# A general path for large experts moves to the end of the program, and the token number scatters to experts 4 to 7

## The chip, the cores and the metric

The kernel runs on one core of a Trainium2 chip. A core has five engines with queues of their own: PE (TensorE, matmuls), ACT (ScalarE), DVE (VectorE), POOL (GpSimd, which here also issues the scatters) and SP (SyncE, which issues the loads). The metric is the device time of one execution in microseconds.

## The reference

Attention runs only between queries and keys whose hashes fall into one bucket. Its output goes token by token to one of eight experts, and the sum of that through a dense layer of two matrices. The hash and softmax of the attention are left out here:

```python
def _moe_ref(x, w_gate, w_output_gate, w1, w2):        # x 1536 x 512, w1 8 x 512 x 1024, w2 8 x 1024 x 512
    e_idx = np.argmax(x @ w_gate, axis=1)
    ...
    for e in range(E):
        mask = e_idx == e
        h = np.maximum(x[mask] @ w1[e], 0.0)
        ye = h @ w2[e]
        out[mask] = gate_w[mask, None] * eom[mask, e, None] * ye

def _moe2_ref(x, w_in, w_out):                         # w_in 512 x 2048, w_out 2048 x 512
    h = x @ w_in
    g = np.where(h > 0.0, h, np.exp(np.minimum(h, 0.0)) - 1.0)
    return g @ w_out
```

## The kernel before

**Attention and gate.** The first third of the program is attention, 16 heads of 768 tokens. At its end the gate picks an expert for each token, ranks the tokens of an expert, and scatters their rows (512 values and the factor) to `xs_d` in DRAM, where each expert has a region of its own. `tab` holds the counts, and as its last number `most`, the largest of them. A path of fixed size takes `CAP` = 224 tokens of each expert; with this data no expert has more.

**Experts.** For expert 0 the tokens are picked with selection matmuls into `xacc`, and ACT and DVE copy that in two halves into the high and low part of `xt`. Expert e+1's rows come from DRAM by `load_xs`, are scaled by POOL (`scale_xs`, L782) and transposed by PE (`make_xT`, tile `xTp`, L1028) inside expert e's second layer. Layer 1 (`moe_L1`, `hps`, L1044) and layer 2 (`moe_L2`, `yps`, L1054) have 96 matmuls of 224 columns each, since every product is made of three: high by high, high by low and low by high. The weights come in 512 KB pieces, `wraw` (eight of an expert, six buffers); ACT makes the high part `wh` (L757) and DVE the low part `wl` (L760). `hh` and `hl` are the two parts of layer 1's output; `hps` has three buffers.

**The general code.** Before expert 0 each engine loads `most` from `tab` (L1060) and branches (L1061) around code that handles what exceeds 224 tokens, with loops over experts and tokens. With this data it is skipped. `keep_warm` (L589) puts 6 matmuls on PE just before it, on data that nobody uses.

**Token numbers.** `tids` scatters, for a quarter of the tokens, their numbers to `tid_d`: three small DVE operations and three indirect DMAs from POOL (L989), with a `spacer` after each. Four groups are called in experts 1 and 2, two in each. `tidt`, loaded from `tid_d`, holds the places of the rows at the end.

**Dense layer and end.** Sixteen blocks `ff_L1`, ELU, `ff_L2` follow, then `finish`: DVE adds to `part` (L1210), and POOL stores it by an indirect DMA through `tidt` (L1214). `lows` issues the subtractions that make `gl`, the low part of the ELU's output.

**What sets the order.** The instructions of each engine stand in the order in which the program is written, each engine runs its own queue in order, and semaphores hold what depends on another engine. SP issues loads as buffers come free, in the order of the program.

Of the kernel before, what the change touches and what calls it, by code (L numbers as in the profile page):

```python
# [17 lines left out]
ENG = mybir.EngineType  # L18
# [7 lines left out]
def kernel(  # L26
# [15 lines left out]
    nc = tc.nc  # L42
    B, H, S, D = q.shape
    E, DM, F = w1.shape
    NT = B * S
# [4 lines left out]
    HC = HALF * 128  # L50
# [44 lines left out]
    PW = KD * F // 4  # L95
    wraw = {}

    def load_piece(pc, e=None):
        i = pc % NP
        we1, we2 = (w1[pc // NP], w2[pc // NP]) if e is None else (w1[bass.ds(e, 1)][0], w2[bass.ds(e, 1)][0])  # L100
        t = raw_p.tile([128, PW], F32, tag="w", name="wraw") if e is None else m1.tile(
            [128, PW], F32, tag="wh", name="wraw", bufs=5
        )
        if i < 4:
            n = F // 4
            src = we1[:, i * n:(i + 1) * n].rearrange("(c p) f -> p c f", p=128)
        else:
            src = we2[:, (i - 4) * 128:(i - 3) * 128].rearrange("(c p) f -> p c f", p=128)
        nc.sync.dma_start(t.rearrange("p (c f) -> p c f", c=src.shape[1]), src)  # L109
        wraw[pc] = t  # L110
# [638 lines left out]
    def split_piece(pc, eng=nc.vector, eng_hi=nc.scalar, rest=None):  # L749
        if pc not in wraw:  # L750
            return
        r = wraw.pop(pc)
        p, a, n = (m2a, "v", 3) if 0 <= pc < 3 else (m1, "w", 5)
        hi = p.tile([128, PW], F32R, tag=a + "h", name="wh", bufs=n)
        lo = p.tile([128, PW], F32R, tag=a + "l", name="wl", bufs=n)
        if eng_hi is nc.scalar:
            eng_hi.activation(hi, r, AF.Copy)  # L757
        else:
            eng_hi.tensor_copy(hi, r)
        fs = [lambda: eng.tensor_tensor(lo, r, hi, ALU.subtract)]  # L760
        if rest is None:
            both(fs)
        else:
            rest.extend(fs)
        wsp[pc] = (hi, lo)
        if pc < 0:
            return
        assert stream[taken[0]] == (pc,)
        taken[0] += 1
        load_ahead()  # L770
# [239 lines left out]
    ps_h = moe.enter_context(tc.tile_pool(name="ps_h", bufs=3, space=PSUM, reuse_waits="tile"))  # L1010


    def load_xs(e, rows=None):
        t = m1.tile([128, 2, XC], F32, tag="xs", name="xs")
        rows = bass.ds(e * REG, ROWS) if rows is None else rows
        nc.sync.dma_start(t, xs_d[rows].rearrange("(t p) d -> p t d", p=128))
        xsl[e] = t

    def make_xT(e, half):
# [36 lines left out]
        nc.scalar.activation(x2h[:, dc, cols], ps, AF.Copy)  # L1056
        nc.vector.tensor_tensor(x2l[:, dc, cols], ps, x2h[:, dc, cols], ALU.subtract)  # L1057

    why = "a count of some of the tokens"
    most = nc.values_load(tab[0:1, 2 * E:2 * E + 1], min_val=0, max_val=NT, skip_runtime_bounds_check_because=why)  # L1060
    with tc.If(most > CAP):  # L1061
        iop = gate_p.tile([128, 2], F32, name="iop")
        nc.gpsimd.iota(iop, pattern=[[128, 2]], base=0, channel_multiplier=1, allow_small_or_imprecise_dtypes=True)
        zrow = m2a.tile([128, XC], F32, tag="mag", name="zrow")
        nc.gpsimd.memset(zrow, 0.0)
        with tc.For_i(0, E, 1) as ev:
            have = nc.values_load(tab[0:1, bass.ds(ev, 1)], min_val=0, max_val=NT, skip_runtime_bounds_check_because=why)
            off = nc.values_load(
                tab[0:1, bass.ds(ev + E, 1)], engines=[ENG.Activation, ENG.DVE], min_val=0, max_val=NT,
                skip_runtime_bounds_check_because=why,  # L1070
            )
            with tc.If(have > CAP):
                tail = gate_p.tile([128, 1], F32, name="tail")
                row = gate_p.tile([128, 2], I32, name="row")
                nc.vector.tensor_tensor(tail, cno[:, 0, bass.ds(ev, 1)], ebase[:, bass.ds(ev, 1)], ALU.add)
                nc.vector.tensor_scalar(row, iop, tail, None, ALU.add)
                for a in range(2):
                    nc.gpsimd.indirect_dma_start(xs_d, bass.IndirectOffsetOnAxis(row[:, a:a + 1], 0), zrow, None)
            with tc.For_i(CAP, have, CAP) as t0:
                load_xs(-1, bass.ds(ev * REG + t0, ROWS))  # L1080
                scale_xs(-1, (nc.scalar, nc.vector))
                make_xT(-1, 0)
                make_xT(-1, 1)
                for f in range(FB1):
                    pc = f // 2 - NP
                    if f % 2 == 0:
                        load_piece(pc, ev)
                        split_piece(pc)
                    moe_L1(-1, f, pc)
                col = nc.s_assert_within(  # L1090
                    off + t0, min_val=0, max_val=NT,
                    skip_runtime_bounds_check_because="t0 is less than what the expert has",
                )
                for dc in range(KD):
                    pc = 4 + dc - NP
                    load_piece(pc, ev)
                    split_piece(pc)
                    moe_L2(-1, dc, pc, col)

    for i in range(1, AHEAD):  # L1100
        split_piece(i)
    for e in range(E):
        if e == 0:
            off = 0
        else:
            off = nc.values_load(
                tab[0:1, E + e:E + e + 1], engines=[ENG.Activation, ENG.DVE], min_val=0, max_val=NT,
                skip_runtime_bounds_check_because="a count of some of the tokens",
            )
        if e == 4:  # L1110
            tidt = gate_p.tile([128, NTT], I32, name="tidt")
            nc.sync.dma_start(tidt, tid_d.rearrange("(t p) o -> p (t o)", p=128))
        if e == 0:
            load_xs(1)
        for f in range(FB1):
            pc = e * NP + f // 2
            moe_L1(e, f, pc)
            narrow_ops(1)
            if f == 1 and e + 1 < E:
                scale_xs(e + 1, (nc.gpsimd, nc.gpsimd))  # L1120
            if f == 2 and 0 < e < 3:
                for gi in range(2 * e - 2, 2 * e):
                    tids(gi)
            if f % 2:
                wsp.pop(pc)
                split_piece(pc + AHEAD)
                if e == E - 1 and f == 7:
                    split_w2(0)
                take_w2()
        if e == 0:  # L1130
            first[0] = False
            load_ahead()
        for dc in range(KD):
# [16 lines left out]
    ps_a = ctx.enter_context(tc.tile_pool(name="ps_a", bufs=1, space=PSUM, reuse_waits="tile"))  # L1150
    m2 = ctx.enter_context(tc.tile_pool(name="m2", bufs=2, reuse_waits="tile"))
    part = [[m2.tile([128, DM], F32, name=f"part{hf}{tt}", bufs=1) for tt in range(2 * HALF)] for hf in range(2)]
    groups = [range(0, W2A), range(W2A, 10), range(10, FB2)]
    steps = [(hf, fb) for g in groups for hf in range(2) for fb in g]
    first_fb, last_fb = [g[0] for g in groups], [g[-1] for g in groups]
# [64 lines left out]
    for k in range(len(steps)):  # L1220
        for j in range(2):
            ps = ff_L1(*steps[k], j)
            if len(todo_w2) < 3:
                take_w2(FB2)
            narrow_ops(3)
            lows()
            ff_elu(*steps[k], j, ps)
            if 0 < k < len(steps) - 1:
                ff_L2(*steps[k - 1], range(HALF * j, HALF * (j + 1)))
            if j == 1 and k + 2 < len(steps) and steps[k + 2][0] == 0 and steps[k + 2][1] > 1:  # L1230
                split_w2(steps[k + 2][1])
    lows()
    for tt in range(2 * HALF):
        for k in (len(steps) - 2, len(steps) - 1):
            ff_L2(*steps[k], [tt])


_INS = [
# [27 lines left out]
```

## Time and profile before

| | |
|---|---|
| median of 3 runs | 743.41 us (743.01 to 743.64) |
| the profiled execution | 745.55 us |
| its span, first to last instruction | 743.8 us |
| mean granted clock of TensorE in it | 0.983 |
| PE busy | 717.9 us, 97% |
| DVE busy | 563.0 us, 76% |
| ACT busy | 400.6 us, 54% |
| POOL busy | 208.9 us, 28% |

The span is that of the one execution that was recorded; the time around it, 1.75 us, has no record. Busy means that a recorded operation ran; branches, semaphores and DMA issues are not counted in it.

### The profile page before, as it was taken

The page shows a single profiled execution, that of the slowest core. Times are in us where ns is not written, and L with a number is a line of the kernel's source. Part 1 is how long each engine was busy: PE and PEld are TensorE (multiplying, and loading weights), DVE is VectorE, ACT ScalarE, POOL GpSimd, SP SyncE. Part 2 cuts the span into 40 slices and gives each one's busy share as a digit, 9 for nine tenths or more (in the row PEclk, how much of TensorE's full clock was granted, in tenths as well). Part 3 has the DMA queues.
Part 4 walks back from the last instruction along what each step waited for, and adds up shares of the span by engine and source line. Part 5 has one row for each costly group of instructions (what it writes and reads, how often), then busy time and mean ns, then how long its engine had stood idle before and what let it go on. Part 6 is the DMA issues. An engine that isn't in the chain of part 4 may idle for free.

```text
span 743.8 us, 13192 instructions
## 1 busy us (share of the span) xinstructions
PE 717.9 (97%) x4686; PEld 674.0 (91%) x4687; DVE 563.0 (76%) x1093; ACT 400.6 (54%) x807; POOL 208.9 (28%) x492
## 2 busy tenths in 40 slices
PE   7999999999999987999999999999999999999996
PEld 5999999999998877999999999889888898899995
DVE  5888898888988975766678898786778965964433
ACT  4897887878878744555555555323433223242221
POOL 7444544454456543154420221100000000000303
PEclk9899999999999988999999999999999999999998
DMA  8856759577582207979898877222112200000202
GB/s 197 192 114 158 187 128 211 150 176 179 136 214 86 72 35 228 267 141 256 182 257 261 263 244 209 83 85 85 58 58 84 79 8 1 0 1 1 85 0 86
DMA packets 108535, 97.74 MB, mean 131 GB/s; under 512 B 33416, under 2 KB 94472, under 8 KB 108464
## 3 DMA queue, kind: packets, MB, share of 16 engines
q1 hardware_dynamic: 106000, 90.44, 46.2%
q0 software_dynamic: 2304, 6.40, 2.3%
q8 instruction: 39, 0.64, 0.4%
q14 instruction: 32, 0.26, 0.1%
q10 hardware_dynamic: 160, 0.00, 0.0%
HBM read 64.15 MB, written 10.72 MB: 101 GB/s over the span
## 4 chain that ended last, share of the span: by engine, by line
issue 40%; PE 12%; DMA 4%; POOL 3%; DVE 1%; ACT 0%; SPq 0%; POOLq 0%; DVEq 0%; ACTq 0%
PE hps L1044 6%; PE yps L1054 5%; DMA xs<-xs_d 4%; POOL xs L782 1%; POOL out_dram L1214 1%; POOL vl L710 1%; PE xTp L1028 1%; DVE wl L760 1%; DVE xTl L1031 0%; ACT wh L757 0%; DVE x2l L1057 0%; SPq L109 0%; POOL spacer L576 0%; ACT x2h L1056 0%; DVE wres L697 0%
## 5 line engine op out<-in xcount | busy, mean ns | idle before, releaser
L367 DVE TENSOR_TENSOR ptlo<-t,pthi 128x384 fp32r<-128x384 f32 x192 | 100.1, 549 | 25.8 <-ACT pthi L366 23.4
L344 ACT ACTIVATE p<-s,bi,sc 128x768 f32<-128x768 f32 x96 | 96.0, 1000 | 21.6 <-POOL bi L337 20.0
L366 ACT ACTIVATE pthi<-t 128x384 fp32r<-128x384 f32 x192 | 84.8, 497 | 25.6 <-PE t L364 24.6
L760 DVE TENSOR_TENSOR wl<-wraw,wh 128x1024 fp32r<-128x1024 f32 x63 | 76.9, 1224 | 21.3 <-ACT wh L757 17.3
L1178 ACT ACTIVATE gh<-ee 128x384 fp32r<-128x384 f32 x64 | 33.7, 526 | 107.8 <-DVE ee L1177 107.8
L335 DVE TENSOR_REDUCE nm<-s 128x1 f32<-128x768 f32 x96 | 91.0, 948 | 0.0
L1166 PE MATMUL gps<-x2l,vh 128*128 128x384 f32 x256 | 86.1, 336 | 0.0
L1166 PE MATMUL gps<-x2h,vh 128*128 128x384 f32 x256 | 86.1, 336 | 0.0
L1166 PE MATMUL gps<-x2h,vl 128*128 128x384 f32 x256 | 85.9, 336 | 0.0
L1214 POOL DMA_INDIRECT out_dram<-part,tidt x12 | 11.6, 969 | 259.0 <-DVE part L1210 256.6
L364 PE MATMUL t<-ident,p 128*128 128x128 f32 x576 | 80.9, 276 | 1.9 <-DVE ptlo L367 1.9
L316 PE MATMUL s<-ka,qa 128*128 128x384 f32 x192 | 74.8, 389 | 3.0 <-ACT p L344 2.4
L1196 PE MATMUL a<-vh,gl 128*128 128x512 f32 x192 | 76.1, 396 | 1.6 <-DVE gl L1179 1.4
L1196 PE MATMUL a<-vh,gh 128*128 128x512 f32 x192 | 75.7, 394 | 0.0
L1196 PE MATMUL a<-vl,gh 128*128 128x512 f32 x192 | 75.6, 394 | 0.0
L364 PEld LDWEIGHTS t<-ident,p 128*128 128x128 f32 x576 | 68.6, 142 | 5.8 <-DVE ptlo L367 2.3
L1054 PE MATMUL yps<-hh,wh 128*128 128x224 f32 x256 | 71.2, 278 | 0.0
L1175 ACT ACTIVATE ee<-gps 128x384 f32<-128x384 f32 x64 | 31.2, 487 | 73.6 <-PE gps L1166 73.3
L1054 PE MATMUL yps<-hl,wh 128*128 128x224 f32 x256 | 70.2, 274 | 0.0
L1054 PE MATMUL yps<-hh,wl 128*128 128x224 f32 x256 | 70.1, 274 | 0.0
L380 PE MATMUL o<-pthi,vst 128*128 128x384 f32 x192 | 68.0, 354 | 0.8 <-ACT osb L401 0.6
L317 PE MATMUL s<-kb,qb 102*128 102x384 f32 x192 | 66.1, 344 | 0.8 <-DVE kb L240 0.8
(202 smaller groups left out, 1872.5 us busy)
## 6 DMA issues: line engine op xcount, KB each, us to landing
wraw<-in_moe_w_dram SPq DMA_DIRECT2D x64, 512.0 KB
w<-in_moe_w_in_dram SPq DMA_DIRECT2D x16, 512.0 KB
w<-in_moe_w_out_dram SPq DMA_DIRECT2D x16, 512.0 KB
ka<-khi SPq DMA_DIRECT2D x30, 192.0 KB
xs_d<-zt SPq DMA_DIRECT2D x8, 528.0 KB
xs<-xs_d SPq DMA_DIRECT2D x8, 528.0 KB
raw_q<-in_q_dram SPq DMA_DIRECT2D x16, 192.0 KB
raw_k<-in_k_dram SPq DMA_DIRECT2D x16, 192.0 KB
```

The lines of the kernel that those rows point to most:

```text
L316: nc.tensor.matmul(ps[:, j, 0:HC], opnd[st, "qa"][:, cb], opnd[st, "ka"][:, sl], start=True, stop=False)
L317: nc.tensor.matmul(ps[:, j, 0:HC], opnd[st, "qb"][0:64 + MROWS, cb], opnd[st, "kb"][0:64 + MROWS, sl], start=False, stop=True,)
L335: nc.vector.tensor_reduce(nm, sps[n][:, :, 0:HC], AX.XY, ALU.max, negate=True)
L344: nc.scalar.activation(p.rearrange("p (a b) -> p a b", a=2), sps.pop(n)[:, :, 0:HC], AF.Exp, bias=bi, scale=sc, accum_out=sums[hd][:, c:c ...
L364: nc.tensor.transpose(ps[:, a, :], p[:, kt * 128:(kt + 1) * 128], ident)
L366: nc.scalar.activation(ho, ps, AF.Copy)
L367: nc.vector.tensor_tensor(lo[:, HALF * g:HALF * (g + 1), i * 128:(i + 1) * 128], ps, ho, ALU.subtract)
L380: nc.tensor.matmul(ops[m], vst[hd][:, kt, :], t[:, kt, :], start=(kt == 0 and x == 0), stop=(kt == NC - 1 and x == 1))
L760: fs = [lambda: eng.tensor_tensor(lo, r, hi, ALU.subtract)]
L1054: nc.tensor.matmul(ps, w[:, f], x[:, f], start=(f == 0 and i == 0), stop=(f == FB1 - 1 and i == 2))
L1166: nc.tensor.matmul(ps, w[:, dc], x[:, dc, c0:c0 + HC], start=(dc == 0 and i == 0), stop=(dc == KD - 1 and i == 2))
L1196: nc.tensor.matmul(ps, x[:, cs], w, start=(fb in first_fb and i == 0), stop=(fb in last_fb and i == 2))
```

## The change

The general code leaves the middle. There POOL alone loads `most` and tests it; the body it would run is two fills of `x2h` and `x2l`. A new general path, `more_tokens`, stands at the end of the program under a test on all engines. It takes 128 rows at a time through both layers of the expert and the dense layer; with this data it is skipped. The token numbers are scattered in experts 4 to 7, one group in each at f == 4, in place of two groups in each of experts 1 and 2 at f == 2, and `tidt` is loaded after the experts. Before the last `lows`, PE takes the last step but one of two parts first. The options that only the general code used leave `load_piece`, `split_piece` and `load_xs`.

```diff
@@ load_piece, split_piece, load_xs: options of the general code removed
-    def load_piece(pc, e=None):
+    def load_piece(pc):
...
-        if pc < 0:
-            return
...
@@ before the loop over experts
-    most = nc.values_load(tab[0:1, 2 * E:2 * E + 1], min_val=0, max_val=NT, skip_runtime_bounds_check_because=why)
+    most = nc.values_load(
+        tab[0:1, 2 * E:2 * E + 1], engines=[ENG.Pool], min_val=0, max_val=NT, skip_runtime_bounds_check_because=more
+    )
     with tc.If(most > CAP):
-        iop = gate_p.tile([128, 2], F32, name="iop")
-        nc.gpsimd.iota(iop, pattern=[[128, 2]], base=0, channel_multiplier=1, allow_small_or_imprecise_dtypes=True)
...
-                    moe_L2(-1, dc, pc, col)
+        nc.gpsimd.memset(x2h.bitcast(F32), 0.0)
+        nc.gpsimd.memset(x2l.bitcast(F32), 0.0)
@@ in the loop over experts
-        if e == 4:
-            tidt = gate_p.tile([128, NTT], I32, name="tidt")
-            nc.sync.dma_start(tidt, tid_d.rearrange("(t p) o -> p (t o)", p=128))
...
-            if f == 2 and 0 < e < 3:
-                for gi in range(2 * e - 2, 2 * e):
-                    tids(gi)
+            if f == 4 and e >= E - NG:
+                tids(e - E + NG)
@@ after it
+    tidt = gate_p.tile([128, NTT], I32, name="tidt")
+    nc.sync.dma_start(tidt, tid_d.rearrange("(t p) o -> p (t o)", p=128))
@@ the dense layer's loop and what follows
                 ff_L2(*steps[k - 1], range(HALF * j, HALF * (j + 1)))
+            elif k and j:
+                ff_L2(*steps[k - 1], [0, 1])
...
     lows()
     for tt in range(2 * HALF):
-        for k in (len(steps) - 2, len(steps) - 1):
+        for k in (len(steps) - 2, len(steps) - 1)[tt < 2:]:
             ff_L2(*steps[k], [tt])
...
+    def more_tokens(e, rows, places):
+        x = raw_tile(XC, "xrow")
+        nc.sync.dma_start(x, xs_d[rows])
...
+        place = gate_p.tile([128, 1], I32, name="place")
+        nc.sync.dma_start(place, tid_d[places])
+        nc.gpsimd.indirect_dma_start(out, bass.IndirectOffsetOnAxis(place, 0), o, None)
+
+    most = nc.values_load(tab[0:1, 2 * E:2 * E + 1], min_val=0, max_val=NT, skip_runtime_bounds_check_because=more)
+    with tc.If(most > CAP):
+        with tc.For_i(0, E, 1) as ev:
...
+                more_tokens(ev, bass.ds(ev * REG + first_row, 128), bass.ds(place0, 128))
```

Two places in the order of the instructions. PE in the middle, before; `warm` is the tile of `keep_warm`, and the dots stand for rows of the general code:

```order
L589 LDWEIGHTS ones_b
L589 MATMUL warm<-ones_b 128x384
L1060 TENSOR_LOAD tab
L1061 COMPARE_AND_BRANCH
...
L1061 UNCONDITIONAL_BRANCH
L1044 MATMUL hps<-xt_4270,wh 128x224
L1044 MATMUL hps<-xt_4271,wh 128x224
```

The same place of the changed kernel, where `hps` is made in L1039; xt_4270 is the high part of xt, xt_4271 the low part:

```order
L587 MATMUL warm<-ones_b 128x384
L1058 UNCONDITIONAL_BRANCH
L587 LDWEIGHTS ones_b
L587 MATMUL warm<-ones_b 128x384
...
L587 LDWEIGHTS ones_b
L587 MATMUL warm<-ones_b 128x384
L1039 MATMUL hps<-xt_4270,wh 128x224
L1039 MATMUL hps<-xt_4271,wh 128x224
```

The load of the count, the compare-and-branch and the code behind it are gone from PE's middle, and one jump stands inside the warm-up.

POOL in the experts, before: the first four scalings of xs (L782) are those for experts 1 and 2, and `tid_d` is written by the token number scatters:

```order
L1061 UNCONDITIONAL_BRANCH
L782 TENSOR_SCALAR xs<-xs 128x512 x4
L989 DMA tid_d<-tok,g_pi 1536x1
L576 MEMSET spacer 1x1
L989 DMA tid_d<-tok,g_pi 1536x1
L576 MEMSET spacer 1x1
```

And of the changed kernel, from its test in the middle on:

```order
L1055 TENSOR_LOAD tab
L1058 COMPARE_AND_BRANCH
L1059 MEMSET x2h 128x7040
L1060 MEMSET x2l 128x7040
L1058 UNCONDITIONAL_BRANCH x2
L778 TENSOR_SCALAR xs<-xs 128x512 x10
L985 DMA tid_d<-tok,g_pi 1536x1
L574 MEMSET spacer 1x1
```

The scatters stand behind ten scalings of xs, those for experts 1 to 5, where they stood behind four.

## Rows read from the trace of the kernel before

**Rows 1.** The chain that ended last, 270 to 300: start us, us, what.

```profile
283.62 13.47 PE hps L1044 x96
```

**Rows 2.** Timeline of PE, 277 to 285: start, us, operation, [idle before <-releaser].

```profile
278.28 1.15 PE L589 MATMUL warm<-ones_b 128*128 128x384 bf16 x6
283.62 0.74 PE L1044 MATMUL hps<-xt,wh 128*128 128x224 f32 x2 [4.19 <-ACT wh L757]
```

**Rows 3.** Instructions of line L1061 by engine: ns min/median/max, first and last start.

```profile
L1061 PEldq EVENT_SEMAPHORE  x2: 51/51/51, 283.2 to 283.4; - x2
...
L1061 PEldq COMPARE_BRANCH x1: 3827/3827/3827, 278.7 to 278.7; - x1
...
L1061 DVEq COMPARE_BRANCH x1: 72/72/72, 281.6 to 281.6; - x1
L1061 POOLq INC_SWDGE_SEM x1: 429/429/429, 282.3 to 282.3; - x1
```

**Rows 4.** Windows of PE: us, busy (instructions), granted clock, DMA share, GB/s.

```profile
283.60:288.90 5.30, 5.28 (x25) 0.50 0.71 200
288.90:297.10 8.20, 8.20 (x75) 1.00 0.84 253
346.80:350.00 3.20, 1.99 (x19) 1.00 1.14 297
```

**Rows 5.** Timelines of ACT and DVE, 277.5 to 287.

```profile
280.20 0.54 ACT L858 ACTIVATE xt<-xacc 128x448 fp32r<-128x448 f32 x1 [1.63 <-PE warm L589]
281.46 2.96 ACT L757 ACTIVATE wh<-wraw 128x1024 fp32r<-128x1024 f32 x3 [0.71 <-ACTq L1060]
...
282.62 3.50 DVE L760 TENSOR_TENSOR wl<-wraw,wh 128x1024 fp32r<-128x1024 f32 x3 [1.22 <-DMA qb<-z]
```

**Rows 6.** PE's waits, 300 to 470: us in total, times, longest.

```profile
PE xTp L1028 <- POOL xs L782: 2.4, 2, 1.2
```

**Rows 7.** The chain that ended last, 320 to 445: loads of xs, issue to landing.

```profile
331.75 12.19 DMA xs<-xs_d
...
423.26 5.68 DMA xs<-xs_d
```

**Rows 8.** Instructions of line L989, the token number scatters.

```profile
L989 POOL DMA_INDIRECT tid_d<-tok,g_pi x12: 955/960/2067, 318.6 to 356.6; - x12
```

**Rows 9.** Windows of the experts, PE busy; the last column is GB/s.

```profile
308.00:318.00 10.00, 10.00 (x92) 1.00 0.89 267
318.00:328.00 10.00, 10.00 (x92) 1.00 0.62 131
328.00:344.00 16.00, 16.00 (x146) 1.00 0.82 185
344.00:354.00 10.00, 8.79 (x80) 1.00 1.09 301
401.00:423.00 22.00, 22.00 (x200) 1.00 0.88 269
```

**Rows 10.** Timeline of PE, 346.5 to 349, the transposes for expert 3.

```profile
346.89 0.27 PE L1028 MATMUL xTp<-ident,xs 128*128 128x128 f32 x1
348.38 0.55 PE L1028 MATMUL xTp<-ident,xs 128*128 128x128 f32 x3 [1.21 <-POOL xs L782]
```

**Rows 11.** Timeline of POOL, 400 to 440, scaling for experts 6 and 7.

```profile
408.16 4.87 POOL L782 TENSOR_SCALAR xs<-xs 128x512 f32<-128x512 f32 x2 [19.85 <-DMA xs<-xs_d]
429.12 3.88 POOL L782 TENSOR_SCALAR xs<-xs 128x512 f32<-128x512 f32 x2 [16.09 <-DMA xs<-xs_d]
```

**Rows 12.** Transposes in 414 to 442: eight for expert 6, four for expert 7.

```profile
L1028 PE MATMUL xTp<-ident,xs x12: 270/272/273, 416.8 to 439.4; 128*128 128x128 f32 x12
```

**Rows 13.** Instructions of line L1214, the stores of the output.

```profile
L1214 POOL DMA_INDIRECT out_dram<-part,tidt x12: 954/960/1038, 687.5 to 738.7; - x12
```

**Rows 14.** Timelines of POOL and DVE, 730 to the end.

```profile
732.41 0.95 POOL L1214 DMA_INDIRECT out_dram<-part,tidt  x1 [37.16 <-DVE part L1210]
...
737.19 0.69 DVE L1210 TENSOR_TENSOR part<-a,part 128x512 f32<-128x512 f32 x1 [0.70 <-PE a L1196]
```

More of the change, by code (lines that the diff above doesn't have):

```diff
@@ L96 @@
     wraw = {}
-    def load_piece(pc, e=None):
+    def load_piece(pc):
         i = pc % NP
[L100 to L103, printed above, removed]
+        we1, we2 = w1[pc // NP], w2[pc // NP]
+        t = raw_p.tile([128, PW], F32, tag="w", name="wraw")
         if i < 4:
@@ L1010, with load_xs @@
     ps_h = moe.enter_context(tc.tile_pool(name="ps_h", bufs=3, space=PSUM, reuse_waits="tile"))
-    def load_xs(e, rows=None):
+    def load_xs(e):
         t = m1.tile([128, 2, XC], F32, tag="xs", name="xs")
-        rows = bass.ds(e * REG, ROWS) if rows is None else rows
-        nc.sync.dma_start(t, xs_d[rows].rearrange("(t p) d -> p t d", p=128))
+        nc.sync.dma_start(t, xs_d[e * REG:e * REG + ROWS].rearrange("(t p) d -> p t d", p=128))
         xsl[e] = t
@@ L1057, in moe_L2 @@
         nc.vector.tensor_tensor(x2l[:, dc, cols], ps, x2h[:, dc, cols], ALU.subtract)
-    why = "a count of some of the tokens"
-    most = nc.values_load(tab[0:1, 2 * E:2 * E + 1], min_val=0, max_val=NT, skip_runtime_bounds_check_because=why)
+    more = "a count of some of the tokens"
+    most = nc.values_load(
+        tab[0:1, 2 * E:2 * E + 1], engines=[ENG.Pool], min_val=0, max_val=NT, skip_runtime_bounds_check_because=more
+    )
     with tc.If(most > CAP):
-        iop = gate_p.tile([128, 2], F32, name="iop")
-        nc.gpsimd.iota(iop, pattern=[[128, 2]], base=0, channel_multiplier=1, allow_small_or_imprecise_dtypes=True)
[L1064 to L1097, printed above, removed]
-                    moe_L2(-1, dc, pc, col)
@@ L1233, with raw_tile, copy, turned @@
     for tt in range(2 * HALF):
-        for k in (len(steps) - 2, len(steps) - 1):
+        for k in (len(steps) - 2, len(steps) - 1)[tt < 2:]:
             ff_L2(*steps[k], [tt])
+    def raw_tile(n, name):
+        return raw_p.tile([128, PW], F32, tag="w", name=name)[:, 0:n]
+    def copy(o, ps):
+        nc.scalar.activation(o, ps, AF.Copy)
+    def turned(src, n, name):
+        dst = raw_tile(n, name)
+        for i in range(0, n, DM):
+            ps = ps_a.tile([128, DM], F32, tag="a0", name="turn")
+            for j in range(0, DM, 128):
+                nc.tensor.transpose(ps[:, j:j + 128], src[:, i + j:i + j + 128], ident)
+            copy(dst[:, i:i + DM], ps)
+        return dst.rearrange("p (c q) -> p c q", q=128)
@@ new lines, in weight_rows @@
+    def weight_rows(src):
+        t = raw_tile(PW, "wrow")
+        nc.sync.dma_start(t.rearrange("p (c n) -> p c n", c=src.shape[1]), src)
+        return t
+    def more_tokens(e, rows, places):
+        x = raw_tile(XC, "xrow")
+        nc.sync.dma_start(x, xs_d[rows])
+        nc.vector.tensor_scalar(x[:, 0:DM], x[:, 0:DM], x[:, DM:DM + 1], None, ALU.mult)
+        xq = turned(x, DM, "xq")
+        ps = [ps_a.tile([128, DM], F32, tag=f"a{1 + i}", name="hrow") for i in range(2)]
+        for dc in range(KD):
+            w = weight_rows(w1[bass.ds(e, 1)][0][dc * 128:(dc + 1) * 128].rearrange("(c p) f -> p c f", c=1))
+            for i in range(2):
+                nc.tensor.matmul(
+                    ps[i], xq[:, dc], w[:, i * DM:(i + 1) * DM], start=(dc == 0), stop=(dc == KD - 1)
+                )
+        h = raw_tile(F, "hrow")
+        for i in range(2):
+            nc.scalar.activation(h[:, i * DM:(i + 1) * DM], ps[i], AF.Relu)
+        hq = turned(h, F, "hq")
+        ps = ps_a.tile([128, DM], F32, tag="a3", name="yrow")
+        for f in range(FB1):
+            if f % 2 == 0:
+                w = weight_rows(w2[bass.ds(e, 1)][0][f * 128:(f + 2) * 128].rearrange("(c p) n -> p c n", p=128))
+            nc.tensor.matmul(ps, hq[:, f], w[:, f % 2 * DM:(f % 2 + 1) * DM], start=(f == 0), stop=(f == FB1 - 1))
+        y = raw_tile(DM, "yrow")
+        copy(y, ps)
+        yq = turned(y, DM, "yq")
+        ps = ps_a.tile([128, DM], F32, tag="a4", name="orow")
+        for fb in range(FB2):
+            for i in range(2):
+                if wide:
+                    load_w2(fb, i)
+                both(narrow_w2(fb, i))
+            wi, wo = wres.pop(fb).rearrange("p a n -> a p n")
+            pg = ps_g.tile([128, HC], F32, tag="g", name="gps")[:, 0:128]
+            for dc in range(KD):
+                nc.tensor.matmul(pg, wi[:, dc * 128:(dc + 1) * 128], yq[:, dc], start=(dc == 0), stop=(dc == KD - 1))
+            ee = m2.tile([128, HC], F32, tag="ee", name="ee")[:, 0:128]
+            nc.scalar.activation(ee, pg, AF.Exp)
+            nc.vector.tensor_scalar(ee, ee, 1.0, 1.0, ALU.min, ALU.subtract)
+            nc.vector.scalar_tensor_tensor(ee, pg, 0.0, ee, ALU.max, ALU.add)
+            nc.tensor.matmul(ps, ee, wo, start=(fb == 0), stop=(fb == FB2 - 1))
+        o = raw_tile(DM, "orow")
+        copy(o, ps)
+        place = gate_p.tile([128, 1], I32, name="place")
+        nc.sync.dma_start(place, tid_d[places])
+        nc.gpsimd.indirect_dma_start(out, bass.IndirectOffsetOnAxis(place, 0), o, None)
@@ new lines @@
+    most = nc.values_load(tab[0:1, 2 * E:2 * E + 1], min_val=0, max_val=NT, skip_runtime_bounds_check_because=more)
+    with tc.If(most > CAP):
+        with tc.For_i(0, E, 1) as ev:
+            have = nc.values_load(tab[0:1, bass.ds(ev, 1)], min_val=0, max_val=NT, skip_runtime_bounds_check_because=more)
+            off = nc.values_load(
+                tab[0:1, bass.ds(ev + E, 1)], engines=[ENG.SP], min_val=0, max_val=NT,
+                skip_runtime_bounds_check_because=more,
+            )
+            with tc.For_i(CAP, have, 128) as t0:
+                first_row = nc.s_assert_within(
+                    have + (CAP - 128) - t0, min_val=0, max_val=NT - 128,
+                    skip_runtime_bounds_check_because="t0 is less than what the expert has",
+                )
+                place0 = nc.s_assert_within(
+                    off + first_row, min_val=0, max_val=NT - 128,
+                    skip_runtime_bounds_check_because="the expert's last token stands among all tokens",
+                )
+                more_tokens(ev, bass.ds(ev * REG + first_row, 128), bass.ds(place0, 128))
```

## The prediction

> **What bounds the kernel now.** I read the chain that ended last first, then the idle time on PE, then the sequencer's own records at the places where PE is idle. From attention's end to the last store the chain lies on PE, so I looked for the few places in the mixture-of-experts stage where PE stands still. There are three. The first is in the middle, at the general code: the warm-up matmuls end at 279.43 (278.28 + 1.15) and the first matmul of expert 0 starts at 283.62, 4.19 us later [rows 2]. The profile puts this down to a high part of a weight piece on ACT, but that engine's record at the place is a load of the count [rows 5], and PE's own record explains the time: its compare-and-branch at 278.7 lasted 3.827 us, where DVE's lasted 0.072 [rows 3]. The reader is to see that the wait is PE's own jump over the general code, not a late operand. The second and third are waits of 1.21 us for the scaled rows of the next expert, 2.4 us together [rows 6].
>
> **The clock behind the gap.** [...] The wait at 348 leaves the clock at 1.00 [rows 4]. So the gap has a second price behind it: expert 0's first layer is 96 matmuls in 13.47 us [rows 1], and at 0.109 it would be 10.50, 2.97 less.
>
> **Edit 1, the general code leaves the middle.** On PE the count load and the compare-and-branch go; what stays is a jump to the next row inside the warm-up. So PE can go straight from 279.43 into expert 0, and 4.19 + 2.97 = 7.16 us are to be had. Something comes due next. ACT has three high parts ahead of its first hh (2.96 us together), and DVE three low parts ahead of its first hl (3.50) [rows 5]; the change leaves both orders as they are. ACT's second copy of xt needs the last selection matmuls, which overlap the start of the warm-up at 278.28 [rows 2]: with its 0.54 us I take 279.1 for its end. The high parts then start at about 279.15, DVE's low parts 1.16 us behind them as now (282.62 against 281.46), so 280.3, and they end at 283.8; hl (0.4) frees the first of three buffers of hps at about 284.2. PE has filled three buffers, 36 matmuls of 0.109, by 283.37. It waits 0.9 us. Term: -4.19 - 2.97 + 0.9 = **-6.3**.
>
> The bound below: if ACT's second copy still starts at 280.20, where the profile shows it 1.63 us behind PE's warm-up matmuls [rows 5], DVE's low half of xt ends about 1.3 us after PE needs it and the first hl is 1.1 us later too; PE loses 1.6 us more, and up to 3 us if the clock falls again. The bound above is no wait at all, -7.2. I take -6.3, since the second copy has no operand that is made after the warm-up begins; only PE's signal of it was late, and PE then stood at the branch.
>
> [...]
>
> POOL's test in the middle: it comes behind the last row scatter on POOL, and the next thing on POOL is scaling xs of expert 1, which waits for its load to land. Nothing waits for the test sooner: zero, with 1 us as the upper bound.
>
> **Edit 2, the token number scatters.** The loads of xs in front of the two PE waits took 12.19 us (the one issued at 331.75) from issue to landing; the one at 423.26 took 5.68 [rows 7]. Between them stand the scatters of tid_d: all 12 lie between 318.6 and 357 in two groups of six [rows 8]. Around the first group the DMA rate falls from 267 GB/s to 131 and then 185 [rows 9], while PE goes on at full pace, so the queues fall behind. Scaled rows come late, and of four transposes in a row the first starts at 346.89, the next three at 348.38 [rows 10], 1.49 us later where matmuls of this kind step by some 0.11. The same again one expert later. With the scatters gone from experts 1 and 2 both waits go: 2 x 1.38 = **-2.8**. Bounds: -2.4 if only the idle time counts [rows 6], and 0 if the landing is late for another reason (the load of weights alone).
>
> They come back as three for each of experts 4 to 7. Price of six, by rate: (259 - 131) x 10 + (259 - 185) x 16 = 2.46 MB not moved, at some 259 GB/s 9.5 us of transfer time (259 is my estimate of the undisturbed demand, a little below the 267 and 269 of [rows 9]). Three should cost about 4.75 us. Catch-up ran at 301 GB/s where expert 6 takes 269 in its undisturbed 22 us [rows 9]: (301 - 269) x 22 = 0.7 MB, or 2.7 us at 259, is won back per expert. What hides the rest: xs of expert 6 is scaled at 413.0 (408.16 + 4.87) and first transposed at 416.8, a margin of 3.8; xs of expert 7 at 433.0 with its first transposes up to 439.4, some 6 [rows 11, 12]. Expert 4's three cost 4.75 against that 3.8 plus what was won back; I take **+0.4**, bounds 0 and, if the price per group doesn't halve, +12 (rival 3). tidt is loaded later, but its first use is the store at 687.5 [rows 13], and nothing reads it sooner: zero. The three small DVE operations per group move with the scatters; DVE has idle time there: zero.
>
> **Edit 3, the end.** POOL paces it: the last six stores begin at 732.41 and 738.7, 1.26 us apart, each 0.96, and the last one's landing stands before the end; DVE's last addition starts at 737.19, before it is needed [rows 13, 14]. Behind the last store POOL now has a count load, a branch and, as in the middle, an INC_SWDGE_SEM of 0.429 us [rows 3]; the load is hidden under the landing. PE's load and branch stand behind its last matmul, which DVE has at 737.19: a branch that starts then and lasts 3.8 us ends at 741.0, under the landing of the store that POOL began at 738.7, and the span ends at 743.8. Term: **+0.5**, bounds 0 and +3.8 (a whole PE branch behind all else).
>
> **Edit 4, the order of the last matmuls.** PE works on other parts while it waits for the last low part. The first addition on DVE still waits for that low part and POOL's pace starts there: zero; the bound is the 0.5 us by which the first store could shift either way. The lost options of the helpers issue the same instructions: zero.
>
> **Sum.** -6.3 - 2.8 + 0.4 + 0.5 = -8.2. Against the profiled execution, 745.55 (span 743.8 and 1.75 around it), that is 737.35. The median of the runs is 2.14 lower than that execution, 743.41, and I carry this over: **735.2**. A measurement tells about 0.2% from no change, 1.5 us: faster is below 741.9, slower above 744.9.
>
> **Rivals.**
> 1. The clock or ACT's copy. PE goes on but stumbles at the start of expert 0, for a copy that PE's late signals held back before. For it: the 1.63 us [rows 5]. Against: no operand is late. Price 1.6 to 4.6: 737 to 740.
> 2. The end pays. PE's branch holds back the signals of its last matmuls, as the 4.19 us show that it holds back what stands behind it; the last addition and store shift by 1.4 to 3.8 us: 736.6 to 739. Against: only matmuls already done stand before it.
> 3. The other side, slower: three scatters cost as much as six, 9.5 us, since what slows the queues may be one burst of descriptors and not their number. Each expert then adds 9.5 - 2.7 = 6.8 of arrears. Expert 5's end is late by 6.8 - 3.8 = 3, expert 6's by 13.6 - 6 - 3 = 4.6 more, and expert 7's weight pieces by what is left, 5 or so: about +12.6, and the time is 735.2 - 0.4 + 12.6 = 747.4. It decides from a loss of 9.7 us on, where it eats the gain beyond 744.9. For it: the delay of 12.19 at 331.75, five us after the group ended. Against: demand there is below the 301 GB/s that the queues reached.
> 4. The change does not do what it says: the jump left in the warm-up stops PE as the branch did. Then edit 1 gives nothing and only edit 2 remains: 743.41 - 2.8 + 0.9 = 741.5, at no measurable difference. Against: its target is the very next row, and a jump of that kind stands today between PE's semaphore steps at 283.4 and the matmul at 283.62 [rows 2, 3], which leaves it 0.2 us at most. [...]
>
> **How the numbers follow.** Forecast (734 to 737) 0.56; rival 1 0.18; rival 2 0.10; rival 3 0.05; rival 4 0.06; better than forecast, with the small waits all zero (733 to 734), 0.05. The range 733.2 to 740.2 takes in rivals 1 and 2 and leaves out 3, 4 and tails. Faster: 0.56 + 0.18 + 0.10 + 0.05 and half of rival 4's, less a little for mishaps: 0.90. Same 0.05, slower 0.05.
>
> **What would show it.** Right: PE's idle time between warm-up and expert 0 below 1 us, with the granted clock at 1.00 through expert 0's first layer, and that layer in some 11.5 us; no PE wait before the transposes in experts 1 and 2; loads of xs in 5 to 8 us there; POOL's last store to the end of the span 5 to 6 us. Wrong: a new PE wait for xs, or for high or low parts, in experts 4 to 7; a clock of 0.50 after the warm-up; PE's compare-and-branch behind the last store in time.

## The result and the profile after

The changed kernel takes 737.12 us (median of 6 runs, 736.25 to 737.45), the kernel before 743.48 beside it (742.12 to 745.71). The ratio is 0.9912, 95% interval 0.9897 to 0.9928: 6.5 us less (5.4 to 7.7). The prediction was 735.2, in a range of 733.2 to 740.2. The profiled execution took 736.89 us, its span is 735.1 and its mean granted clock 0.987.

The timeline of PE in the middle, after:

```profile
279.04 1.15 PE L587 MATMUL warm<-ones_b 128*128 128x384 bf16 x6
279.89 0.58 PE L1039 MATMUL hps<-xt,wh 128*128 128x224 f32 x2
...
284.61 0.49 PE L1039 MATMUL hps<-xt,wh 128*128 128x224 f32 x2 [0.34 <-DVE hl L1041]
```

Expert 0's first matmul starts before the recorded end of the last warm-up matmul (280.19); the 4.19 us of [rows 2] are gone. The one wait left, 0.34 us at 284.61, is the predicted one for the first buffer of hps behind DVE's three low parts (0.9 was predicted). A window and the chain that ended last, after:

```profile
280.19:291.50 11.31, 10.97 (x97) 1.00 0.89 273
```

```profile
291.57 5.36 PE yps L1049 x48
...
303.16 10.72 PE hps L1039 x96
...
325.46 10.72 PE hps L1039 x96
...
347.77 10.72 PE hps L1039 x96
...
370.08 10.72 PE hps L1039 x96
```

The clock is 1.00 throughout expert 0's first layer, where [rows 4] had 0.50 in its first 5.30 us. From the start of the warm-up to that of layer 2 it takes 291.57 - 279.04 = 12.53 us; before it was 283.62 + 13.47 - 278.28 = 18.81 [rows 1, 2]. That is 6.28 less. In the chain each layer 1 starts 22.3 us after the one ahead, in experts 2 to 4 too: the two waits of [rows 6] are gone. Line L1265, the test at the end, and the end of POOL's and DVE's timelines, after:

```profile
L1265 PEldq COMPARE_BRANCH  x1: 3962/3962/3962, 724.4 to 724.4; - x1
...
L1265 POOLq INC_SWDGE_SEM  x1: 887/887/887, 729.7 to 729.7; - x1
```

```profile
729.72 0.96 POOL L1174 DMA_INDIRECT out_dram<-part,tidt  x1 [0.22 <-POOLq L1265]
...
728.02 0.69 DVE L1170 TENSOR_TENSOR part<-a,part 128x512 f32<-128x512 f32 x1 [0.67 <-PE a L1156]
```

PE's branch takes 3.96 us there as well, from 724.4 to 728.4: it begins while the last matmuls still run, and PE has nothing left to do behind it. From the start of the last store to the end of the span it is 735.1 - 729.72 = 5.4 us; before it was 743.8 - 738.7 = 5.1 [rows 13].

The two traces differ by 8.7 us and the medians by 6.4. Later traces of either kernel show how far one execution differs from the next.

### The profile page after: what moved, and what is told of

Its sections match the earlier page's. It is cut to its first block, busy times and chain, and to the rows that moved or that the text cites. A ratio compares the mean times of both kernels' runs of the same rounds, so it can differ in the third digit from the quotient of the medians.

```text
span 735.1 us, 13186 instructions
## 1 busy us (share of the span) xinstructions
PE 714.1 (97%) x4686; PEld 672.0 (91%) x4687; DVE 562.6 (77%) x1093; ACT 400.3 (54%) x807; POOL 206.9 (28%) x492
## 3 DMA queue, kind: packets, MB, share of 16 engines
HBM read 64.15 MB, written 10.72 MB: 102 GB/s over the span
## 4 chain that ended last, share of the span: by engine, by line
PE 50%; issue 31%; DMA 9%; DVE 4%; ACT 3%; POOL 1%; SPq 1%; ACTq 0%; POOLq 0%; DVEq 0%
PE yps L1049 10%; PE hps L1039 10%; PE o L378 8%; PE t L362 7%; DMA out_dram<-part,tidt 6%; PE s L314 4%; PE s L315 4%; PE zps L229 2%; PE sp L454 2%; ACT p L342 1%; PE prep L203 1%; DMA tid_d<-tok,g_pi 1%; PE xTp L1023 1%; DMA qb<-qhi 1%; PE xacc L818 1%
```

## The experiments

They ran in three groups, each on a chip of its own with the kernel before beside them: its medians were 745.66, 746.39 and 743.80. Comparisons stay within a group or use the ratio to the kernel before. In the table the stretches (us) are from each run's own trace, cut at the starts of PE's matmuls: warm-up to layer 2 of expert 0, from there to the first matmul of the dense layer, from there to its last matmul, and from that to the end of the span.

| run | ratio to before (95%) | warm-up to layer 2 | experts | dense | end |
|---|---|---|---|---|---|
| before, first trace | 1 | 18.65 | 169.81 | 270.02 | 7.05 |
| before again | 1.001 (0.9993 to 1.0028) | 17.92 | 173.06 | 269.96 | 7.06 |
| middle only | 0.9932 (0.9906 to 0.9958) | 12.37 | 168.38 | 270.33 | 7.06 |
| token numbers only | 0.9974 (0.9960 to 0.9988) | 18.06 | 168.35 | 270.01 | 7.08 |
| changed, first trace | 0.9912 (0.9897 to 0.9928) | 12.37 | 166.86 | 269.32 | 7.53 |
| changed, second | 0.9877 (0.9853 to 0.9900) | 12.37 | 167.66 | 269.29 | 7.52 |
| changed, third | 0.9924 (0.9906 to 0.9941) | 14.06 | 167.31 | 269.31 | 7.52 |
| no end path | 0.9889 (0.9868 to 0.9910) | 12.37 | 167.77 | 270.36 | 7.04 |
| old matmul order | 0.9875 (0.9852 to 0.9899) | 12.37 | 167.99 | 269.33 | 7.54 |
| PE tests, one matmul | 0.9904 (0.9882 to 0.9925) | 12.36 | 168.53 | 269.39 | 7.20 |
| PE tests, 120 matmuls | 0.9979 (0.9964 to 0.9994) | 16.08 | 168.37 | 269.39 | 7.21 |
| six in experts 5 and 6 | 0.9984 (0.9968 to 1.0000) | 12.74 | 174.51 | 269.31 | 7.57 |
| numbers in dense | 0.9895 (0.9871 to 0.9919) | 12.37 | 166.86 | 270.95 | 7.50 |
| numbers late in dense | 0.9982 (0.9968 to 0.9995) | 14.11 | 166.86 | 274.07 | 7.52 |

(The table starts a stretch at the first record of a matmul, a few hundredths of a us off the grouped rows above.)

**The kernel before, again** (no edit).

> The kernel before, unchanged, to see how much one execution differs from the next. The two traces differ by 8.7 us, the medians of the runs by 6.4. Theory A (the terms of the prediction hold in every execution): a new profile shows the 4.2 us gap in the middle, about 25 matmuls at half clock and two waits of 1.2 us for xs, with a span near 743.8. Theory B (the first profiled execution was a slow one of its kind): the span is near 741.7, and the place that is shorter than in the first trace (clock, xs, or something outside the change) is where the 2.1 us went.

It took 746.87 us where its neighbour took 745.66, the same within the interval. PE's waits, 275 to 470, and the landing of two loads of xs in the chain:

```profile
PE xTp L1028 <- POOL xs L782: 3.9, 3, 1.4
PE hps L1044 <- PEq L1061: 3.1, 1, 3.1
```

```profile
335.26 7.80 DMA xs<-xs_d
...
353.05 15.18 DMA xs<-xs_d
```

A window of PE behind the second and third of these waits, at 370.55 and 372.10:

```profile
372.10:377.00 4.90, 4.90 (x29) 0.65 1.15 305
```

The places are those of the prediction, their sizes change from one execution to the next. The gap is 3.1 us in place of 4.19: the branch's record is 3.50 us in place of 3.83, and PE's semaphore steps follow it at once, where they came some 0.6 us later in the first trace [rows 3]; why they did, no run shows. The waits for xs are 3.9 us in place of 2.4, and here the clock falls behind them, to 0.65 in that window. The prediction had read from the wait at 348 that they leave the clock at 1.00 [rows 4] and gave them no price of this kind; the experts take 3.25 us more than in the first trace, of which 1.5 are longer waits. The span, 745.3, is near that of Theory A and not the 741.7 of Theory B, but the sizes do vary, as B had it: the terms are always there, and a single trace of the kernel before sizes them only to 1 or 3 us.

**The middle alone, and the token numbers alone.**

```diff
@@ middle only: before, with the body and the engines of the test as changed
-    most = nc.values_load(tab[0:1, 2 * E:2 * E + 1], min_val=0, max_val=NT, ...)
+    most = nc.values_load(tab[0:1, 2 * E:2 * E + 1], engines=[ENG.Pool], ...)
@@ token numbers only: before, with
-            if f == 2 and 0 < e < 3:
-                for gi in range(2 * e - 2, 2 * e):
-                    tids(gi)
+            if f == 4 and e >= E - NG:
+                tids(e - E + NG)
```

> Before, with the general code in the middle gone and POOL's test alone in its place; token numbers, end and order of the last matmuls as before. The general path is left out altogether. Theory A: 6.3 us less than before (737.1), no gap between warm-up and expert 0, clock at 1.00, both waits for xs still there with loads of 12 us. Theory B with the clock as the part that varies: some 4 us less (739.4). If the token numbers alone made the gain: 743.4.

> Before, with only the token number scatters moved to experts 4 to 7 and tidt loaded after the experts; the general code stays in the middle. Theory A: 2.9 us less (740.5), no wait of PE for xs in any expert, gap in the middle unchanged. Theory B with the waits for xs as the part that varies between executions: 0 to 1 us less (742.5 to 743.4) although the trace shows no wait. Rival (the load of weights alone makes xs late): the waits stay and the time is 743.4.

The middle alone gives 0.68% or 5.1 us (3.1 to 7.0) of 745.66 where 6.3 was expected, the token numbers 0.26% or 1.9 us (0.9 to 3.0) where 2.9 was. Neither gain is zero, which ends both "only one of them" readings, and their sum, 7.0, lies within the 5.7 to 9.2 us of the changed kernel's three comparisons. PE's waits, 275 to 470, of the middle alone and then of the token numbers alone:

```profile
PE xTp L1028 <- POOL xs L782: 1.3, 1, 1.3
```

```profile
PE hps L1044 <- PEq L1061: 3.4, 1, 3.4
PE xTp L1028 <- POOL xs L782: 0.8, 1, 0.8
PE hps L1044 <- DVE xTl L1031: 0.3, 1, 0.3
```

With the middle alone one early wait for xs stays (two were expected), with the token numbers alone none does; but a wait of 0.8 comes at the transposes for expert 7, behind the scatters of the experts ahead. The times of the middle alone lie in two clusters, three from 737.95 to 738.78 and four from 741.65 to 742.95, and its trace is of the first. Its 168.38 us in the experts, as good as the 168.35 with the scatters moved, does not speak for the second cluster; the gain of the token numbers rests on the times and not on these two traces. The second and third trace of the changed kernel give 0.8 and 0.45 us more in the experts than the first; in the second PE waits 0.6 us for xs at the transposes for expert 7, in the third for no xs. The two runs further down that scatter in the dense layer have the first trace's 166.86. The new place is not free in every execution.

**No end path, and the old order of the last matmuls.**

```diff
@@ no end path: changed, without
-    most = nc.values_load(tab[0:1, 2 * E:2 * E + 1], min_val=0, max_val=NT, ...)
-    with tc.If(most > CAP):
...
@@ old matmul order: changed, with
-            elif k and j:
-                ff_L2(*steps[k - 1], [0, 1])
...
-        for k in (len(steps) - 2, len(steps) - 1)[tt < 2:]:
+        for k in (len(steps) - 2, len(steps) - 1):
```

> The changed kernel without the general path and its test at the end; the rest is as changed. My term for the end: 0.5 us less than the changed kernel (736.6 against 737.1), with the last store to the end of the span in 4.1 us as before and not 4.4. Rival (PE's branch of 3.96 us holds the end): 1.4 us or more less, below 735.7.

> The changed kernel with the last matmuls in the order of before. My term is zero: same time as the changed kernel within 0.5 us, first addition and first of the last six stores at the same distance from the end. Rival: the new order fills a wait of PE for the last low part, so that undoing it costs 0.5 us.

Without the end path the last matmul stands 7.04 us from the end, as before (7.05); with it 7.5. Counted from the end of the last store's record, as the expectation does, it is 4.1 us without and 4.4 with the path. The term of 0.5 holds and the rival of 1.4 or more falls. The times can't show 0.5 us. The old order changes nothing: 737.72 beside 737.38 for the changed kernel in that group, with overlapping intervals, and the same end.

**Why PE's branch was dear.** PE too loads and tests the count, and skips a body of `n` matmuls on a tile of its own:

```diff
@@ changed, with n = 1 and n = 120
-        tab[0:1, 2 * E:2 * E + 1], engines=[ENG.Pool], min_val=0, ...
+        tab[0:1, 2 * E:2 * E + 1], engines=[ENG.Pool, ENG.PE], min_val=0, ...
+        idle = ps_y.tile([128, CAP], F32, tag="y", name="idle")
+        for i in range(n):
+            nc.tensor.matmul(idle[:, 0:128], ones_b, ones_b, start=(i == 0), stop=(i == n - 1))
```

> The changed kernel, but PE too loads and tests the count in the middle, and skips a body of a single matmul in place of some 200 rows. If the price is that of the jump's distance: the branch takes well under 1 us and the time is that of the changed kernel. If it is that of a taken branch on PE whatever it skips: 3.5 to 3.9 us of branch, a gap of 3 to 4.2 us, low clock behind it and 4.5 to 6.3 us more, near 743.

> As the run in which PE tests the count and skips one matmul (its branch took 0.233 us), but the skipped body has 120 matmuls with their weight loads, 240 rows. If the jump's distance makes the price: a branch of 3.5 to 3.9 us as in the kernel before, a gap of 3 to 4.2 us and low clock behind it, 4.5 to 6.3 us more than the changed kernel. If it was the general code's loops and the waits at its end, and not its length: a branch of about 0.2 us and the time of the short body.

The branch and what PE does next, with one matmul to skip:

```profile
L1058 PEldq COMPARE_BRANCH  x1: 233/233/233, 279.6 to 279.6; - x1
```

```profile
280.57 0.45 PE L1039 MATMUL hps<-xt,wh 128*128 128x224 f32 x2 [0.30 <-PEq L1058]
```

The same, and the clock behind it, with 120 (240 rows):

```profile
L1058 PEldq COMPARE_BRANCH  x1: 353/353/353, 280.3 to 280.3; - x1
```

```profile
283.52 0.64 PE L1039 MATMUL hps<-xt,wh 128*128 128x224 f32 x2 [2.52 <-ACT wh L755]
```

```profile
283.50:286.00 2.50, 2.48 (x12) 0.52 0.50 161
```

One skipped matmul costs PE 0.30 us and nothing of the clock (warm-up to layer 2 in 12.36, as in the changed kernel; the time, 739.10 beside 737.38, has an overlapping interval). 240 skipped rows cost 2.52 us and bring the clock to 0.52 behind; warm-up to layer 2 takes 3.7 us longer than with one. The time is 0.9979 of before, against 0.9924 for the changed kernel in the same group: most of the gain is gone. Apart from the chip the two runs differ in the skipped body alone, so how much code is jumped over is what costs, and not the load or the test. The sizes were expected larger: a branch of 3.5 to 3.9 us (it is 0.353), a gap of 3 to 4.2 (2.52) and 4.5 to 6.3 us more than the changed kernel (3.8). The branch record itself is short here, where it held 3.83 us before: the wait can stand in the record or behind it, and the first matmul's idle time is what to read. The DMA queues point to what PE waits for: the part on packets of code, 277 to 286, of the kernel before and then of the 240 rows:

```profile
q8 instruction: 2, 0.03, 1.8%
q14 instruction: 5, 0.04, 1.5%
```

```profile
q8 instruction: 1, 0.02, 0.9%
```

In that window the changed kernel and the run with one matmul have no such packet. With the 240 rows it is under way from 281.4 to 282.8, between the end of PE's branch at 280.7 and PE's next step at 283.3. The packets bear no engine's name; that this one is PE's is read from its time. The traces line up: no packet and 0.30 us with one matmul, one packet and 2.52 us with 120, and in the two traces of the kernel before, where all five engines branch, seven packets and 4.19 and 3.1 us. That PE's wait is the loading of its code is an inference from these numbers, which no run shows by itself; nor does one show from how many rows on, between two and 240, a jump is dear.

**Number and place of the scatters.**

```diff
@@ six in experts 5 and 6
-            if f == 4 and e >= E - NG:
-                tids(e - E + NG)
+            if f == 4 and e in (5, 6):
+                tids(2 * e - 10)
+                tids(2 * e - 9)
@@ numbers in dense: instead, in the loop over k
+        if 10 <= k < 10 + NG:
+            tids(k - 10)
+        if k == 18:
+            tidt = gate_p.tile([128, NTT], I32, name="tidt")
...
@@ numbers late in dense: in the loop over j, and tidt at k == 20
+            if 17 <= k < 19:
+                tids(2 * (k - 17) + j)
```

> The changed kernel again, unchanged, as the measure for the other runs of this call and to see which of its stretches differ between executions. Theory: between warm-up and expert 0 and in the transposes it repeats itself (no wait over 0.5 us), so its times spread less than those of the kernel before. Rival: the three scatters per expert make a wait of about 1 us for xs or for weights in experts 5 to 7 in some executions, as the runs with the new place have shown (0.9 and 0.55 us).

> The changed kernel with the four groups of token numbers in the dense layer (steps 10 to 13) and tidt loaded at step 18, where the load of weights is far below that in the experts. Theory (the scatters' price is contention with the weight loads, 0 to 1.5 us now): no wait of PE in any expert, and 0 to 1.5 us less than the changed kernel. Rival (the price is nothing): the same time. Other side: POOL or DVE come late in the dense layer and it is slower.

> The changed kernel with two groups of token numbers, six scatters, in each of experts 5 and 6 at f == 4, in place of one in each of 4 to 7. Theory (number in a row decides, and the delay does not come with the place): waits for xs of 1 to 1.5 us in front of the transposes for experts 7 and of weights or xs near them, 1.5 to 3 us more than the changed kernel. Rival (the place decides, experts 5 to 7 have slack enough): no wait over 1 us and the same time.

> The changed kernel with the four groups of token numbers in steps 17 and 18 of the dense layer, one per half step, where DVE has idle time of 0.6 to 2 us before each operation, and tidt loaded at step 20. Theory: neither a wait for xs in the experts nor late low parts in the dense layer; 0.5 to 1.5 us less than the changed kernel. Rival: POOL's scatters or SP's load of tidt come too late for the first stores, or the low parts wait again: same or slower.

> The changed kernel once more, as the measure for the other runs of this call: 737.1 to 737.4, a wait of 0 to 0.8 us for xs or weights in experts 5 to 7, none in experts 1 to 3, no low clock behind the warm-up.

Six in a row in experts 5 and 6 take 743.24 us beside 738.59 for the changed kernel: 4.7 us more, where 1.5 to 3 were expected, and 7.2 more in the trace's experts. The number in a row decides, as the theory said, and the late experts' slack doesn't cover six. The mechanism was not the one expected, though. PE doesn't wait for xs; it waits for xT's low parts. One of ACT's waits of that run, 395 to 450, one of PE's, 275 to 470, and two windows of PE behind it:

```profile
ACT x2h L1051 <- remote: 6.7, 2, 3.5
```

```profile
PE hps L1039 <- DVE xTl L1026: 2.6, 2, 1.6
```

```profile
417.30:422.00 4.70, 4.64 (x27) 0.64 1.16 186
443.60:448.00 4.40, 4.34 (x27) 0.68 0.80 85
```

ACT stands still twice, 6.7 us in all (a wait at that place is usually 1.4), for something that the trace does not name, and DVE and PE come late behind it. PE's waits are only 2.6 us. Behind each of them the clock falls: 27 matmuls take 4.64 and 4.34 us, which at 0.112 each (96 in 10.72 us in the chain of the changed kernel) would be 3.0, so that some 3 us more go there.

With the scatters in the dense layer the experts take 166.86 us in both traces, as in the first of the changed kernel, and more is lost behind them; 0.5 to 1.5 us less was expected of the late place, 0 to 1.5 of the other. In steps 10 to 13 of the dense layer's 32 DVE has little room (in the changed kernel it is busy for 29.2 us of the 35 from 541 to 576); PE waits 1.8 us for its low parts from 530 to 580, in place of 0.6, and the layer is 1.6 us longer (738.77 beside 737.38 in that group, intervals overlapping). Late in the dense layer DVE has room (7.1 us busy of the 18 from 600 to 618 in the changed kernel), and it is worse: 742.77 beside 738.59. The timeline of ACT there, and the DMA queues, 608 to 620:

```profile
618.43 0.49 ACT L1131 ACTIVATE ee<-gps 128x384 f32<-128x384 f32 x1 [5.31 <-PE a L1152]
```

```profile
DMA packets 259, 0.04 MB, mean 3 GB/s; under 512 B 256, under 2 KB 256, under 8 KB 256
...
q14 instruction: 2, 0.02, 3.2%
q8 instruction: 1, 0.02, 1.9%
q0 software_dynamic: 256, 0.00, 1.6%
```

And of the changed kernel, the 12 us around the same code, 603 to 615, where nothing is scattered:

```profile
q8 instruction: 1, 0.02, 0.7%
q14 instruction: 1, 0.01, 0.2%
```

A share of 3.2% of 16 engines in 12 us is 6.1 us for two packets of code, 3.1 each; alone such a packet takes 0.4 (0.2%). The large one takes 3.6 in place of 1.3. All this at 3 GB/s. ACT's wait of 5.31 us falls into the same stretch (2.12 is usual at that place); that it waited for its code was not tried by a run of its own. In steps 20 to 23 DVE has little room again (26.8 us busy of the 34 from 626 to 660 in the changed kernel), and the delay is carried on: PE waits 1.86 us for a low part at 644.07, and the clock behind it reads 0.61 from 644.0 to 648.4. The dense layer takes 274.07 in place of 269.3. No version beat the changed kernel.

In the third trace of the changed kernel ACT's copy of xt was late again:

```profile
281.15 0.54 ACT L854 ACTIVATE xt<-xacc 128x448 fp32r<-128x448 f32 x1 [1.59 <-remote]
```

```profile
281.75 0.37 PE L1039 MATMUL hps<-xt,wh 128*128 128x224 f32 x1 [0.60 <-ACT xt L854]
```

## Why the prediction was right, point by point

**The gap and the clock** (-6.3): the first traces gave 6.28, the times of the middle alone 5.1 (3.1 to 7.0). The two runs that bring PE's test back show the cause, the code that the jump skips; that its loading is the wait rests on the packets. The clock went with the gap: 0.52 behind 2.52 us, 1.00 behind 0.30. The 2.97 us of the term are the 13.47 of [rows 1] less 96 matmuls at 0.109 each, which is 75 in 8.20 us in the second window of [rows 4], at a clock of 1.00; in the first window, at 0.50, 25 take 5.28. With the change 96 take 10.72 us in experts 1 to 4, 0.112 each. The wait for hps was 0.34 and not 0.9. DVE's timeline, after:

```profile
280.76 3.50 DVE L758 TENSOR_TENSOR wl<-wraw,wh 128x1024 fp32r<-128x1024 f32 x3 [0.18 <-ACT wh L755]
284.17 0.68 DVE L1041 SCALAR_TENSOR_TENSOR hl<-hps,hh 128x224 fp32r<-128x224 f32 x2
```

The warm-up starts 0.76 us later in this trace (279.04 against 278.28), so the times are counted from there. DVE's low parts began 1.72 us after it and not 2.0, and PE went on at 5.57, where the first hl was worked out for 5.9. PE's first 36 matmuls began 0.3 us earlier than worked out but took 4.4 us and not 3.9, and were done 0.14 later. Both shorten the wait.

**A step whose reason failed.** I took ACT's second copy as on time, "since the second copy has no operand that is made after the warm-up begins; only PE's signal of it was late, and PE then stood at the branch". It is late by 1.59 us in the third trace of the changed kernel, where PE has no branch, and on time (0.99 us for both copies) in the second trace of the kernel before, where it has. In all it is late in four of the fourteen traces, two with PE's branch and two without; so the lateness does not need the branch. Rival 1 is then a matter of the execution: where it happens it costs 1.7 us (14.06 against 12.37; 14.11 in the run with the numbers late in the dense layer), close to its lower price of 1.6, and the clock stays at 1.00.

**The token numbers** (-2.8 and +0.4): the two early waits went in the first trace, and alone the edit measures 1.9 us (0.9 to 3.0). The +0.4 is 0 to 0.8 us in the three traces of the changed kernel. That the waits for xs can bring the clock down too, to 0.65 in the second trace of the kernel before, the term put at nothing. I priced the scatters by the bytes that other transfers did not move; the runs do not bear that account out. With six in a row the price shows in ACT's wait and the clock, and late in the dense layer three packets of code grow to several times their length (3.1 and 3.6 us in place of 0.4 and 1.3) with the DMA engines nearly idle (3 GB/s). Rival 3 fell as it was put: three in a row do not cost as much as six, which in the late experts take the gain away (0.9984). Its thought that bytes are not what counts fits the runs.

**The end** (+0.5): 7.53 against 7.05. Rival 2 fell: PE's 3.96 us of branch began ahead of the last matmul and ran under the stores, and DVE's last addition starts 0.43 us after the last matmul's start in both traces. **The last matmuls' order** (0): nothing seen.

**Rival 4** fell with the run that skips one matmul, and with the changed kernel, whose jump in the warm-up leaves no wait.

**The term that was mis-sized** is the last one: "The median of the runs is 2.14 lower than that execution, 743.41, and I carry this over". The profiled execution of the changed kernel took 736.89, which is 0.46 under the 737.35 of my sum, and its runs have their median there, at 737.12. So the 2.14 belonged to the kernel before alone; without it the forecast would have been 737.35. The likely reading is that its profiled execution lost more in the very places that the change removes, and that I took this off twice: the sizes there do change from trace to trace (17.92 to 18.65 in the middle, 2.4 to 3.9 us of waits for xs), and the gain goes from 0.76% to 1.23% over the three comparisons of the changed kernel (5.7 to 9.2 us). The clocks on record point the same way. The profiled execution has a mean granted clock of 0.983; of the 64 executions of the kernel before in the three groups the 17 at 0.983 or less have a median of 746.5 us, the 26 at 0.986 or more one of 743.8. So an execution that takes longer spends more time at the low clock. In which places it does, these numbers do not tell, and no execution of before at 743.4 has a trace: that it was those that the change removes is argued and not shown.

That the sum without the carry-over, 737.35, lies within 0.3 us of the measured median is partly luck: measured alone, the two main terms are 5.1 and 1.9, with intervals 3.9 and 2.1 us wide, where the sum had 6.3 and 2.4.

## What to carry to other kernels

Here a jump over 240 rows cost PE 2.52 us and one over two rows 0.30, though the code behind it never ran. So put a branch over much code where the engine whose queue is full has nothing left to do (PE's branch of 3.96 us at the end is part of a path that costs 0.5), or test on an engine with slack (POOL in the middle), and look at the idle time behind it and at the packets of code, not only at the record of the branch (0.353 us where the idle time was 2.52). In this kernel scatters of single words were priced by how many stood in a row (six took 4.7 us more than three) and by what came late behind them, not by their bytes. A wait has a second price where the clock falls behind it (0.50 behind the 4.19 us, 0.65 behind waits for xs of 1.41 and 1.22); one trace in which it stays at 1.00 does not rule that out. Where one trace stands above its kernel's median, ask whether the difference lies in what the change removes before carrying it over.

## What the runs showed that I had not expected

Packets of code took 3.1 and 3.6 us in place of 0.4 and 1.3 while POOL scattered words of four bytes at 3 GB/s in all. ACT waited 0.9 to 3.5 us, in three traces (at xt in two of them, twice at x2h in the third; at x2h 1.4 us of each are usual), for something that the trace calls remote; the cause stays open. And the dense layer takes 269.3 us in all traces that hold the general path at the end and are otherwise undisturbed there, 270.0 to 270.4 in the five without it, so that the path costs 0.5 at the end (0.2 in the two runs in which PE tests in the middle too, 7.21) and comes with 0.6 to 1.1 less ahead of it; why, no run shows.
